# Attention into two gated layers on one core: block transposes moved from TensorE to VectorE and DRAM

## Chip, cores and metric

The kernel runs on one core of one Trainium2 chip. The metric is the device time in microseconds (us) of one execution. Of the kernel before, three runs gave 1791.05, 1791.21 and 1791.79 us; the median is 1791.21.

## What is computed

The inputs are q, k and v of shape (8, 8, 576, 64): batch B, heads H, sequence S, head width D. Linear attention is followed by two feed-forward layers on 4608 tokens of width 512:

```python
q_s = exp(q - max(q, -1)); q_s = q_s / (sum(q_s, -1) + 1e-9)
k_s = exp(k - max(k, 2));  k_s = k_s / (sum(k_s, 2) + 1e-9)
kv  = einsum('bhsd,bhse->bhde', k_s, v)
x   = einsum('bhsd,bhde->bhse', q_s, kv)       # then (B, H, S, D) -> (B*S, H*D)
x   = (silu(x @ w_gate) * (x @ w_val)) @ w_out     # d_ff 1536
out = elu(x @ w_in) @ w_out2                       # d_ff 2048
```

The maximum and the sum over the keys run over the sequence, which lies on partitions in the kernel; the queries' run over the head width, which lies along a partition.

## The kernel before

The tokens are cut into NB = 9 blocks of TB = 512. Every matrix of the feed-forward layers is kept as a high and a low float32r part, and a product is three matmuls (`proj`, lines 617 to 640, and `mm3`, lines 609 to 615). The program has three phases over the nine blocks: "a" (first half of w_gate, w_val, w_out), "b" (second half) and "2" (the second layer).

In phase a, block i has HALF = 6 steps f, and each step has three slots s. Slot 0 is the gate projection, followed on ScalarE (ACT) by the four operations of `silu_act` (lines 660 to 663). Slot 1 is the value projection, with `silu_gate` (lines 667 and 670) and `silu_val` (line 673) on VectorE (DVE). Slot 2 is the w_out product of the step before (`emit_B`). Two PSUM tiles "a" alternate between gate and value, so the gate projection of step f+1 needs line 670 of step f to be done. The low part of the activated tile is line 651 on DVE.

Beside this, block i prepares the attention of block t = i+1. What runs in which slot is written by hand: `PLAN0`, `PLAN1` and `PLAN` (lines 784 to 805) give every step a pair (f, s) for i = 0, i = 1 and i from 2 on; `steps` (line 808) says what a step is; `side_1a` (line 849) issues those of a slot in the order of the plan's text. Each engine, and SP's queue of DMAs, runs in that order of issue. The steps that matter here:

- `load_k`, `load_q`, `load_v` (lines 227 to 265) load keys, queries and values. The values go in five DMAs with rows of 256 bytes (line 242), issued with `kv1`; the queries go in rows of 1024 bytes. A query tile has partition p holding tokens 4p to 4p+3 of the block.
- `kmax` (267) takes the key maximum over the tokens of one partition. `k1` (276) turns it with four TensorE transposes (line 280) into a PSUM bank and reduces it on DVE (284). `k2` (289) broadcasts it back with four transposes (line 293) into another bank, and `ks` (305) subtracts it from the keys. `kexp` (314) takes the exponent on ACT, `kv` (322) multiplies keys and values in 80 small matmuls (line 331) and divides on DVE.
- `qmax`, `qsub`, `qexp`, `qsum`, `qnorm` (350 to 381) make the query softmax. `qnorm` writes the tile `qn` (line 378).
- `qT` (385) turns one pair of heads with four TensorE transposes (line 390) into a bank and copies it on ACT into a tile `qT` (line 398). There are four pairs. `xT` (412) multiplies two pairs with the kv product (`xT_mm`, line 451), copies to the tile x on ACT (433) and takes the low part on DVE (463).
- `store` (468) writes x to DRAM for phase b.

The transposed token order is that of the tile, so `emit_D` writes the output rows as `(p j)` of a block. Lines 390 and 293 and the matmuls of lines 331 and 451 use the two PSUM banks "t" and "c".

Of the kernel before, what the change touches and what calls it, by code (L numbers as in the profile page):

```python
# [17 lines left out]
def kernel(  # L18
# [184 lines left out]
    k_t, q_t, km_t = {}, {}, {}  # L203


    ke = at1.tile([128, 5, H, D], FP32, name="ke")
    start = [True]

# [28 lines left out]
    def load_v(b):  # L237
        for j in range(5):
            n = 128 if j < 4 else NREST
            src = v[b, :, 0:512, :].rearrange("h (p j) d -> p j h d", j=4)[:, j] if j < 4 else \  # L240
                v[b, :, 512:S, :].rearrange("h p d -> p h d")
            nc.sync.dma_start(out=vtile[0:n, j, :, 0:D], in_=src)  # L242


    def load_q(t):
        qt = at1.tile([128, H, 4, D], FP32, tag="q", name="q")
        p0 = min(16 * t, 128)
        s0 = TB * t
        if p0 > 0:
            b = t - 1  # L250
            s = s0 - b * S
            for e in range(2):
                nc.sync.dma_start(
                    out=qt[0:p0, 4 * e:4 * e + 4],
                    in_=q[b, e::2, s:s + 4 * p0, :].rearrange("h (p j) d -> p h (j d)", j=4),
                )
        if p0 < 128:
            b = t
            s = s0 + 4 * p0 - b * S
            for e in range(2):  # L260
                nc.sync.dma_start(
                    out=qt[p0:128, 4 * e:4 * e + 4],
                    in_=q[b, e::2, s:s + 4 * (128 - p0), :].rearrange("h (p j) d -> p h (j d)", j=4),
                )
        q_t[t] = qt

    def kmax(b):
        t, r = k_t[b]
        m = at1.tile([128, H, D], FP32, tag="km", name="km")
        nc.vector.tensor_tensor(m, t[:, :, 0, :], t[:, :, 1, :], op=ALU.max)  # L270
        nc.vector.tensor_tensor(m, m, t[:, :, 2, :], op=ALU.max)
        nc.vector.tensor_tensor(m, m, t[:, :, 3, :], op=ALU.max)
        nc.vector.tensor_tensor(m[0:NREST], m[0:NREST], r, op=ALU.max)
        km_t[b] = m

    def k1(b, meanwhile=None):
        m = km_t[b].rearrange("p h d -> p (h d)")
# [36 lines left out]
    def kexp(b):  # L314
        nc.scalar.activation(out=ke[:, 0:4], in_=ke[:, 0:4], func=ACTF.Exp)
        nc.scalar.activation(out=ke[0:NREST, 4], in_=ke[0:NREST, 4], func=ACTF.Exp)
# [53 lines left out]
    def qnorm(t, n, eng=None):  # L370
        h = slice(4 * n, 4 * n + 4)
        x = q_t[t][:, h]
        r = qr_t[t][:, h]
        nc.vector.tensor_scalar(r, r, 1e-9, None, op0=ALU.add)
        nc.vector.reciprocal(out=r, in_=r)
        if n == 0:
            qn_t[t] = at1.tile([128, 4, H, D], FP32, tag="qn", name="qn")
        (eng or nc.vector).tensor_tensor(
            qn_t[t][:, :, h].rearrange("p j h d -> p h j d"), x,
            r.unsqueeze(3).to_broadcast([128, 4, 4, D]), op=ALU.mult,  # L380
        )

    qT_t = {}

    def qT(t, pair):
        g, e = divmod(pair, 2)
# [54 lines left out]
    def xT_mm(t, g, banks):  # L441
        p0 = min(16 * t, 128)
        for b, c in ((t - 1, slice(0, p0)), (t, slice(p0, 128))):
            if c.start == c.stop:
                continue
            for e in range(2):
                pair = 2 * g + e
                for a, ps in banks.items():
                    r = slice(a * D, (a + 1) * D)
                    o = slice(e * D, (e + 1) * D)  # L450
                    nc.tensor.matmul(  # L451
                        out=ps.rearrange("p (j n) -> p j n", j=4)[o, :, c],
                        lhsT=bds[b % 2][r, pair, :],
                        rhs=qT_t[t, pair].rearrange("p (j n) -> p j n", j=4)[r, :, c],
                        start=True, stop=True,
                    )
        for a, ps in banks.items():
            xT_ps[t, 2 * g + a] = ps
# [285 lines left out]
    def emit_D(i, f):  # L744
        if f == 0:
            acc_tiles(("2", i))
        gt = G.pop((i, f))
        w = W["p", f]
        for j in range(4):
            js = slice(j * 128, (j + 1) * 128)  # L750
            mm3(acc["2", i][j], (gt[:, 0, js], gt[:, 1, js]), (w[:, 0, :], w[:, 1, :]),
                f == 0, f == F2 - 1)
        if f == F2 - 1:
            ev = ev_p.tile([128, KD, TB], FP32, tag="ev", name="ev")
            dst = out[i * TB:(i + 1) * TB, :].rearrange("(p j) n -> p j n", j=4)
            for j in range(4):
                if i == NB - 1 and j == 3:
                    nc.scalar.activation(
                        out=ev[:, j, 0:256], in_=acc["2", i][j][:, 0:256], func=ACTF.Copy
                    )  # L760
                    nc.vector.tensor_copy(ev[:, j, 256:512], acc["2", i][j][:, 256:512])
                elif j % 2 == 0:
                    nc.scalar.activation(out=ev[:, j, :], in_=acc["2", i][j], func=ACTF.Copy)
                else:
                    nc.vector.tensor_copy(ev[:, j, :], acc["2", i][j])
                if i == NB - 1:
                    nc.sync.dma_start(out=dst[:, j], in_=ev[:, j])
            if i < NB - 1:
                nc.sync.dma_start(out=dst, in_=ev)
# [4 lines left out]
    def load_next(ph, i):  # L774
# [7 lines left out]


    PLAN = {
# [4 lines left out]
        "kmax": (4, 2), "qmax": (5, 2),  # L789
    }  # L790
    PLAN0 = {
# [13 lines left out]
        "kmax": (4, 2), "qmax": (5, 2),  # L805
    }

    def steps(i):
        t, u = i + 1, i + 2
        e = nc.gpsimd if i == 0 else nc.vector  # L810
        st = {}
        if i == 1:
            st["store0"] = lambda: store_x(0)
        if t < B:
            st["kmax0"] = lambda: kmax(t)
            st["k1"] = lambda: k1(t)
            st["k2"] = lambda: (k2(t), t + 1 < B and t > 1 and load_k(t + 1))
            st["ks0"] = lambda: ks(t, (0, 1), nc.gpsimd)
            st["ks1"] = lambda: (ks(t, (2, 3), nc.gpsimd), ks(t, (4,), nc.vector))
            st["load_v"] = lambda: load_v(t)  # L820
            st["load_k2"] = lambda: load_k(t + 1)
            st["load_q2"] = lambda: load_q(t + 1)
            st["load_v2"] = lambda: load_v(t + 1)
            st["kexp"] = lambda: kexp(t)
            st["kv0"] = lambda: kv(t, 0)
            st["kv1"] = lambda: (
                kv(t, 1),
                t + 1 < B and t > 1 and load_v(t + 1),
            )
        if t < NB:  # L830
            st["qmax0"] = lambda: (qmax(t, 0), qmax(t, 1))
            st["sub0"] = lambda: qsub(t, 0, e)
            st["sub1"] = lambda: qsub(t, 1, e)
            st["exp0"] = lambda: qexp(t, 0)
            st["exp1"] = lambda: qexp(t, 1)
            st["sum"] = lambda: (qsum(t, 0), qsum(t, 1))
            st["norm0"] = lambda: qnorm(t, 0, e)
            st["norm1"] = lambda: (qnorm(t, 1, e), t + 1 < NB and t > 1 and load_q(t + 1))
            for n in range(KD):
                st[f"qT{n}"] = lambda n=n: qT(t, n)  # L840
                st[f"xT{n}"] = lambda n=n: xT(t, n)
            st["store"] = lambda: store_x(t)
        if u < B:
            st["kmax"] = lambda: kmax(u)
        if u < NB:
            st["qmax"] = lambda: (qmax(u, 0), qmax(u, 1))
        return st
# [90 lines left out]
    with tc.manual_schedule():  # L938
        nc.gpsimd.memset(ident, 1.0)
        nc.gpsimd.affine_select(  # L940
            out=ident, in_=ident, pattern=[[-1, 128]], compare_op=ALU.is_equal, fill=0.0,
            base=0, channel_multiplier=1,
        )
        warm = const.tile([128, 1], FP32, name="warm")
        nc.vector.memset(warm, 0.0)
        nc.scalar.activation(out=warm, in_=warm, func=ACTF.Exp)
        first_block()
        start[0] = False
        run_1()
        run_2()  # L950
# [30 lines left out]
```

## Time and profile before

| | us |
|---|---|
| median of three runs | 1791.21 |
| the profiled execution | 1792.23 |
| its span in the trace | 1790.5 |
| TensorE busy / DVE busy / ACT busy | 1752.0 / 924.9 / 856.0 |

PE is the matmul side of TensorE and PEld its weight loads. Times in rows are us from the start of the span. A timeline row gives start, duration, engine, line, operation, output and inputs with shapes, count, and in brackets the idle time before it with what ended it. A window row gives the busy time of each engine with the number of instructions, then the granted TensorE clock as a share of full speed, the mean busy share of the 16 DMA engines (which can pass 1 where transfers overlap) and GB/s. In a DMA issue row the last number is the median time from issue to landing.

### The profile page before, as it was taken

How to read it: one execution, taken by the hardware profiler on the slowest of the kernel's cores; microseconds unless marked ns; L12 is line 12 of the kernel's file. 1: busy time of each engine (PE TensorE's matmuls, PEld its weight loads, DVE VectorE, ACT ScalarE, POOL GpSimd, SP SyncE). 2: the span in 40 equal slices, each digit the busy share in tenths (PEclk: the TensorE clock that was granted, in tenths of full speed). 3: DMA queues.
4: the chain of work that ended last, by engine and by line, in shares of the span. 5: the costliest groups of instructions: out<-in, count | busy, mean ns of one | idle time of the engine just before them, and what ended most of it. 6: DMA issues, size and time to landing. Idle time of an engine off the chain costs nothing.

```text
span 1790.5 us, 21046 instructions
## 1 busy us (share of the span) xinstructions
PE 1752.0 (98%) x8448; PEld 1433.3 (80%) x8448; DVE 924.9 (52%) x1383; ACT 856.0 (48%) x1466; POOL 173.1 (10%) x135
## 2 busy tenths in 40 slices
PE   6799999999999999999999999999999999999999
PEld 4577888888888888888888788888888888888887
DVE  6866567556577666534346744333433343334343
ACT  4563544534465454433334654444444444444444
POOL 3630000000022222111113300000000000000000
PEclk9899999999999999999999999999999999999999
DMA  9274534341255344433334401010101010101000
GB/s 273 80 228 102 147 100 124 105 114 65 78 192 176 129 171 168 165 118 118 118 118 164 174 3 71 1 71 1 71 1 71 1 71 1 71 1 71 1 24 24
DMA packets 103106, 169.13 MB, mean 94 GB/s; under 512 B 41696, under 2 KB 80608, under 8 KB 98528
## 3 DMA queue, kind: packets, MB, share of 16 engines
q1 hardware_dynamic: 103008, 167.79, 28.5%
q8 instruction: 66, 1.08, 0.3%
q14 instruction: 32, 0.26, 0.0%
HBM read 111.15 MB, written 56.62 MB: 94 GB/s over the span
## 4 chain that ended last, share of the span: by engine, by line
PE 90%; issue 2%; DVE 2%; POOL 2%; ACT 2%; DMA 1%; SPq 1%; POOLq 0%; DVEq 0%; ACTq 0%
PE a L632 17%; PE a L633 17%; PE a L636 17%; PE y L613 12%; PE y L615 12%; PE y L614 12%; POOL w L183 1%; PE t L451 1%; DMA ev<-in_v 1%; PE t L390 1%; SPq L242 0%; PE t L331 0%; PE c L331 0%; DMA xs<-x 0%; POOL ke L310 0%
## 5 line engine op out<-in xcount | busy, mean ns | idle before, releaser
L632 PE MATMUL a<-x,w 128*128 128x512 f32 x1432 | 562.8, 393 | 1.5 <-DVE th L688 1.2
L633 PE MATMUL a<-x,w 128*128 128x512 f32 x1432 | 558.9, 390 | 0.7 <-POOL x L463 0.7
L636 PE MATMUL a<-x,w 128*128 128x512 f32 x1432 | 382.8, 389 | 0.0
L645 ACT ACTIVATE g<-th 128x512 fp32r<-128x512 f32 x252 | 159.3, 632 | 442.4 <-DVE th L673 226.3
L632 PEld LDWEIGHTS a<-x,w 128*128 128x128 f32 x1432 | 269.8, 188 | 60.7 <-DVE th L688 2.0
L633 PEld LDWEIGHTS a<-x,w 128*128 128x128 f32 x1432 | 269.8, 188 | 56.2 <-POOL x L463 1.2
L636 PEld LDWEIGHTS a<-x,w 128*128 128x128 f32 x1432 | 268.8, 188 | 55.8
L685 DVE SCALAR_TENSOR_TENSOR th<-e,th 128x512 f32<-128x512 f32 x144 | 100.9, 701 | 356.6 <-ACT e L684 356.6
L651 DVE TENSOR_TENSOR g<-th,g 128x512 fp32r<-128x512 f32 x246 | 176.2, 716 | 136.7 <-ACT g L645 136.6
L613 PE MATMUL y<-w,g 128*128 128x512 f32 x576 | 224.1, 389 | 0.0
L615 PE MATMUL y<-w,g 128*128 128x512 f32 x576 | 224.1, 389 | 0.0
L614 PE MATMUL y<-w,g 128*128 128x512 f32 x576 | 224.1, 389 | 0.0
L667 DVE SCALAR_TENSOR_TENSOR th<-th,e 128x512 f32<-128x512 f32 x108 | 77.3, 715 | 274.6 <-ACT th L663 274.6
L682 ACT ACTIVATE e<-a 128x512 f32<-128x512 f32 x144 | 86.1, 598 | 183.4 <-PE a L636 183.4
L613 PE MATMUL y<-g,w 128*128 128x512 f32 x432 | 171.8, 398 | 0.0
L660 ACT ACTIVATE e<-a 128x512 f32<-128x512 f32 x107 | 64.1, 599 | 224.4 <-PE a L636 224.3
L614 PE MATMUL y<-g,w 128*128 128x512 f32 x432 | 169.0, 391 | 0.0
L615 PE MATMUL y<-g,w 128*128 128x512 f32 x432 | 169.0, 391 | 0.0
L183 POOL TENSOR_TENSOR w<-cd,w 128x512 fp32r<-128x512 f32 x68 | 91.6, 1349 | 624.8 <-ACT w L182 604.1
L613 PEld LDWEIGHTS y<-w,g 128*128 128x128 f32 x576 | 108.2, 188 | 22.6
L615 PEld LDWEIGHTS y<-w,g 128*128 128x128 f32 x576 | 108.1, 188 | 22.5
L614 PEld LDWEIGHTS y<-w,g 128*128 128x128 f32 x576 | 108.1, 188 | 22.3
(137 smaller groups left out, 1705.7 us busy)
## 6 DMA issues: line engine op xcount, KB each, us to landing
xs<-x SPq DMA_DIRECT2D x9, 2048.0 KB, 6.3
x<-xs SPq DMA_DIRECT2D x36, 512.0 KB, 6.2
ys<-yst SPq DMA_DIRECT2D x36, 512.0 KB, 3.7
x<-ys SPq DMA_DIRECT2D x36, 512.0 KB, 7.2
raw<-in_moe_w_out SPq DMA_DIRECT2D x26, 512.0 KB, 3.3
yp<-ev SPq DMA_DIRECT2D x9, 1024.0 KB, 4.0
ev<-yp SPq DMA_DIRECT2D x9, 1024.0 KB, 7.9
raw<-in_moe_w_in SPq DMA_DIRECT2D x16, 512.0 KB, 4.0
```

The lines of the kernel that those rows point to most:

```text
L183: eng.tensor_tensor(w[:, 1, :], df, w[:, 0, :].bitcast(FP32), op=ALU.subtract)
L613: nc.tensor.matmul(out=ps, lhsT=wh, rhs=xh, start=first, stop=False)
L614: nc.tensor.matmul(out=ps, lhsT=wh, rhs=xl, start=False, stop=False)
L615: nc.tensor.matmul(out=ps, lhsT=wl, rhs=xh, start=False, stop=last)
L632: nc.tensor.matmul(out=ps, lhsT=wh, rhs=x[:, c, 0, :], start=(c == 0), stop=False)
L633: nc.tensor.matmul(out=ps, lhsT=wh, rhs=x[:, c, 1, :], start=False, stop=False)
L636: nc.tensor.matmul(out=ps, lhsT=wl, rhs=x[:, c, 0, :], start=False, stop=(c == KD - 1))
L645: nc.scalar.activation(out=gt[:, 0, :], in_=src, func=ACTF.Copy)
L651: (eng or nc.vector).tensor_tensor(gt[:, 1, :], src, gt[:, 0, :].bitcast(FP32), op=ALU.subtract)
L667: nc.vector.scalar_tensor_tensor(out=t, in0=t, scalar=1.0, in1=e, op0=ALU.add, op1=ALU.mult)
L682: nc.scalar.activation(out=e, in_=h, func=ACTF.Relu, scale=-1.0)
L685: nc.vector.scalar_tensor_tensor(out=t, in0=e, scalar=1.0, in1=t, op0=ALU.add, op1=ALU.mult)
```

## The change

From block TURN = 3 on, TensorE does no transposes for the attention.

- Queries: `qnorm` now scales in place. `qturn` turns 32x32 squares of the query tile on DVE, two instructions of 128x512 elements for each half of the heads, and writes them so that the token order is natural. `qout` writes the tile to a DRAM tensor `dq` in four DMAs, each from 32 partitions with rows of 512 bytes, 1 MB in all. `qin` reads two pairs at a time back as tiles `qT`, two DMAs of 256 KB with rows of 2 KB. `xT_mm` uses plain column slices for these blocks.
- Key maxima: `kturn` turns the 128x512 tile on DVE into a PSUM bank, reduces, turns again, copies and reduces again on DVE, writes 16x32 values to DRAM and reads them back broadcast to 128 partitions.
- `PLAN` is written anew: the softmax of the queries and keys moves up by one to three slots, `turn1` (which issues `qout`, `qin(t, 0)` and the next query load) stands in slot (2, 0) behind `kv1`, `xT0` and `xT1` stay in (3, 1), `in1` follows them there, and `xT2` and `xT3` move from (4, 1) to (4, 2). The copies of line 398, the second PSUM tile of the key maxima and lines 280, 293 and 390 are gone for these blocks.
- `emit_D` writes rows of blocks 3 to 8 as `(j p)`.

```diff
+    TURN = 3
+    NQ = 32
+    dq = {t: dr.tile([KD, 4, NQ, 4, 128], FP32, name=f"dq{t}") for t in range(TURN, NB)}
+    dk = {b: dr.tile([2 * H, NQ], FP32, name=f"dk{b}") for b in range(TURN, B)}
...
+    def kturn(b):
+        m = km_t[b].rearrange("p h d -> p (h d)")
+        ps = bank()
+        nc.vector.transpose(ps, m)
+        nc.vector.tensor_reduce(
+            out=kq[:, 0:2 * H], in_=ps.rearrange("p (x c) -> p x c", c=NQ), axis=AX.X, op=ALU.max
+        )
+        nc.vector.transpose(kt_, kq)
+        for g in range(4):
+            nc.vector.tensor_copy(kc[:, g], kt_[g * NQ:g * NQ + 2 * H])
+        mk = at2.tile([2 * H, NQ], FP32, tag="mk", name="mk")
+        nc.vector.tensor_reduce(
+            out=mk, in_=kc.rearrange("p g r -> p r g"), axis=AX.X, op=ALU.max
+        )
+        nc.sync.dma_start(out=dk[b], in_=mk)
+        mb = at1.tile([128, H, D], FP32, tag="km", name="mb")
+        nc.sync.dma_start(
+            out=mb.rearrange("p h d -> p (h d)"),
+            in_=dk[b].rearrange("x r -> (x r)").unsqueeze(0).to_broadcast([128, H * D]),
+        )
+        km_t[b] = mb
...
+        if t >= TURN:
+            nc.vector.tensor_tensor(
+                x, x, r.unsqueeze(3).to_broadcast([128, 4, 4, D]), op=ALU.mult
+            )
+            return
...
+    def qturn(t, n):
+        if n == 0:
+            qn_t[t] = at1.tile([128, 2 * H, 128], FP32, tag="qn", name="qn")
+        h = slice(4 * n, 4 * n + 4)
+        for e in range(2):
+            o = qn_t[t].rearrange("p (h e) (c j) -> p h e j c", e=2, j=4)[:, h, e]
+            nc.vector.transpose(o, q_t[t][:, h, :, e * NQ:(e + 1) * NQ])
+
+    def qout(t):
+        for g in range(4):
+            nc.sync.dma_start(
+                out=dq[t].rearrange("s q r g n -> r (s q) g n")[:, :, g],
+                in_=qn_t[t][g * NQ:(g + 1) * NQ],
+            )
+
+    def qin(t, g):
+        for e in range(2):
+            x = at2.tile([128, 512], FP32, tag="qT", name="qT")
+            nc.sync.dma_start(
+                out=x, in_=dq[t][2 * e + g].rearrange("q r g n -> (q r) (g n)")
+            )
+            qT_t[t, 2 * g + e] = x
...
     PLAN = {
-        "k1": (0, 1), "k2": (1, 0), "kexp": (1, 0), "kv0": (2, 0), "kv1": (2, 0),
-        "sub0": (0, 2), "exp0": (0, 2), "sub1": (0, 2), "exp1": (0, 2), "sum": (1, 2), "norm0": (2, 1), "norm1": (2, 2),
-        "qT0": (3, 0), "qT1": (3, 0), "xT0": (3, 1), "xT1": (3, 1),
-        "qT2": (4, 0), "qT3": (4, 0), "xT2": (4, 1), "xT3": (4, 1), "store": (5, 0),
-        "kmax": (4, 2), "qmax": (5, 2),
+        "sub0": (0, 0), "exp0": (0, 0), "sub1": (0, 0), "exp1": (0, 0),
+        "ks": (0, 2), "kexp": (0, 2), "sum": (1, 0), "norm0": (1, 1), "norm1": (1, 2),
+        "turn0": (1, 2), "kv0": (2, 0), "kv1": (2, 0), "turn1": (2, 0),
+        "xT0": (3, 1), "xT1": (3, 1), "in1": (3, 1), "xT2": (4, 2), "xT3": (4, 2), "store": (5, 1),
+        "kmax": (4, 1), "kturn": (4, 2), "qmax": (5, 2),
     }
...
+            st["ks"] = lambda: (
+                ks(t, range(5), nc.vector), t + 1 < B and load_k(t + 1),
+            )
...
-            st["norm1"] = lambda: (qnorm(t, 1, e), t + 1 < NB and t > 1 and load_q(t + 1))
+            st["norm1"] = lambda: (qnorm(t, 1, e), t + 1 < NB and t == 2 and load_q(t + 1))
+            st["turn0"] = lambda: qturn(t, 0)
+            st["turn1"] = lambda: (
+                qturn(t, 1), qout(t), qin(t, 0), t + 1 < NB and load_q(t + 1),
+            )
+            st["in1"] = lambda: qin(t, 1)
```

`PLAN1` gets `"kturn": (5, 0)`. In `kv1` the next value load stays as it was, for t from 2 to 6.

## Rows read from the trace of the kernel before

**Rows 1.** The page, parts 1 and 4: busy times, and shares of the chain.

```profile
span 1790.5 us, 21046 instructions
...
PE 1752.0 (98%) x8448; PEld 1433.3 (80%) x8448; DVE 924.9 (52%) x1383; ACT 856.0 (48%) x1466; POOL 173.1 (10%) x135
...
PE 90%; issue 2%; DVE 2%; POOL 2%; ACT 2%; DMA 1%; SPq 1%; POOLq 0%; DVEq 0%; ACTq 0%
```

**Rows 2.** Windows, one block of phase a (i = 4) nearly whole.

```profile
297.00:354.00 57.00, 57.00 (x354) 46.28 (x353) 35.70 (x57) 26.90 (x47) 0.00 (x0) 1.00 0.41 117
```

**Rows 3.** Timeline of PE in that block, from step f = 2 to step f = 3.

```profile
300.84 0.39 PE L632 MATMUL a<-x,w 128*128 128x512 f32 x1
...
311.72 0.39 PE L632 MATMUL a<-x,w 128*128 128x512 f32 x1
...
313.53 1.07 PE L636 MATMUL a<-x,w 128*128 128x512 f32 x4
314.44 0.60 PE L390 MATMUL c<-ident,qn 128*128 128x128 f32 x4
...
317.16 1.07 PE L636 MATMUL a<-x,w 128*128 128x512 f32 x4
318.15 0.48 PE L451 MATMUL t<-qT,bd 64*64 64x320 f32 x1
```

**Rows 4.** Timeline of ACT: the ends of three gate projections, steps 5, 0 and 2.

```profile
392.18 0.60 ACT L660 ACTIVATE e<-a 128x512 f32<-128x512 f32 x1 [2.47 <-PE a L636]
400.34 0.60 ACT L660 ACTIVATE e<-a 128x512 f32<-128x512 f32 x1 [3.13 <-PE a L636]
...
417.60 0.60 ACT L660 ACTIVATE e<-a 128x512 f32<-128x512 f32 x1 [2.33 <-PE a L636]
```

**Rows 5.** Timeline of DVE: qnorm to the next product, and the key subtractions.

```profile
365.10 0.17 DVE L374 TENSOR_SCALAR qr<-qr 128x16 f32<-128x16 f32 x1
...
366.73 0.68 DVE L673 SCALAR_TENSOR_TENSOR th<-th,a 128x512 f32<-128x512 f32 x1
...
409.40 2.48 DVE L310 TENSOR_TENSOR ke<-k,t 128x512 f32<-128x512 f32 x4 [1.42 <-PE t L293]
411.80 0.67 DVE L312 TENSOR_TENSOR ke<-kr,t 64x512 f32<-64x512 f32 x1
```

**Rows 6.** Timeline of SP's queue: the value load of block i = 4.

```profile
305.78 4.20 SPq L242 DMA_DIRECT2D vtile<-in_v  x5
```

**Rows 7.** Windows: values; their end; queries from 32 partitions; keys.

```profile
310.50:311.00 0.50, 0.50 (x4) 0.42 (x3) 0.43 (x3) 0.47 (x1) 0.00 (x0) 1.00 1.34 218
312.00:312.50 0.50, 0.50 (x4) 0.42 (x3) 0.50 (x2) 0.00 (x0) 0.00 (x0) 1.00 0.97 124
316.50:317.00 0.50, 0.50 (x4) 0.42 (x3) 0.21 (x1) 0.50 (x2) 0.00 (x0) 1.00 1.08 219
358.00:359.00 1.00, 1.00 (x6) 0.84 (x5) 1.00 (x2) 0.35 (x1) 0.00 (x0) 1.00 1.08 386
```

**Rows 8.** The page, part 6: DMA issues to and from DRAM.

```profile
xs<-x SPq DMA_DIRECT2D x9, 2048.0 KB, 6.3
...
raw<-in_moe_w_out SPq DMA_DIRECT2D x26, 512.0 KB, 3.3
yp<-ev SPq DMA_DIRECT2D x9, 1024.0 KB, 4.0
```

**Rows 9.** Waits of PE (total us, times, longest), early in the run.

```profile
PE t L331 <- ACT ke L315: 3.1, 1, 3.1
...
PE t L390 <- ACT xf L436: 1.2, 1, 1.2
```

**Rows 10.** Windows: after the 3.1 us wait, and around the 1.2 us wait.

```profile
76.00:80.00 4.00, 4.00 (x32) 3.30 (x30) 2.55 (x4) 4.00 (x9) 3.13 (x3) 0.57 0.00 0
98.00:100.00 2.00, 0.87 (x6) 0.83 (x7) 0.69 (x1) 1.25 (x3) 2.00 (x2) 1.00 1.14 241
```

More of the change, by code (lines that the diff above doesn't have):

```diff
@@ L203 @@
     k_t, q_t, km_t = {}, {}, {}
+    TURN = 3
+    NQ = 32
+    dq = {t: dr.tile([KD, 4, NQ, 4, 128], FP32, name=f"dq{t}") for t in range(TURN, NB)}
+    dk = {b: dr.tile([2 * H, NQ], FP32, name=f"dk{b}") for b in range(TURN, B)}
+    kq = at1.tile([128, NQ], FP32, name="kq")
+    kt_ = at1.tile([128, NQ], FP32, name="kt")
+    kc = at1.tile([2 * H, 4, NQ], FP32, name="kc")
     ke = at1.tile([128, 5, H, D], FP32, name="ke")
@@ L450, in xT_mm @@
                     o = slice(e * D, (e + 1) * D)
+                    x = qT_t[t, pair]
+                    if t >= TURN:
+                        c4 = slice(4 * c.start, 4 * c.stop)
+                        out_, rhs = ps[o, c4], x[r, c4]
+                    else:
+                        out_ = ps.rearrange("p (j n) -> p j n", j=4)[o, :, c]
+                        rhs = x.rearrange("p (j n) -> p j n", j=4)[r, :, c]
                     nc.tensor.matmul(
[L452 to L455, printed above, removed]
+                        out=out_, lhsT=bds[b % 2][r, pair, :], rhs=rhs, start=True, stop=True,
                     )
@@ L754, in emit_D @@
             ev = ev_p.tile([128, KD, TB], FP32, tag="ev", name="ev")
-            dst = out[i * TB:(i + 1) * TB, :].rearrange("(p j) n -> p j n", j=4)
+            dst = out[i * TB:(i + 1) * TB, :]
+            if i >= TURN:
+                dst = dst.rearrange("(j p) n -> p j n", j=4)
+            else:
+                dst = dst.rearrange("(p j) n -> p j n", j=4)
             for j in range(4):
@@ L804 @@
         "qT2": (4, 0), "qT3": (4, 1), "xT2": (4, 2), "xT3": (4, 2), "store": (5, 2),
-        "kmax": (4, 2), "qmax": (5, 2),
+        "kmax": (4, 2), "kturn": (5, 0), "qmax": (5, 2),
     }
@@ L844, in steps @@
             st["kmax"] = lambda: kmax(u)
+            st["kturn"] = lambda: kturn(u)
         if u < NB:
@@ L945 @@
         nc.vector.memset(warm, 0.0)
+        nc.vector.memset(kq, 0.0)
         nc.scalar.activation(out=warm, in_=warm, func=ACTF.Exp)
```

## The prediction

> **What bounds the kernel now.** I read the page first: PE is busy 1752.0 of 1790.5 us and carries 90% of the chain that ended last, while DVE is busy 52% and ACT 48% [rows 1]. Shares are averages, so the next view is the windows of one block of phase a: PE is busy for the whole 57 us, DVE for 35.7, and the granted clock is 1.00 [rows 2]. In this stretch every instruction taken from PE shortens the run, and every wait put in front of PE lengthens it; DVE and ACT have room. So the timeline of PE tells the gain, and the queue of SP and the windows of the DMA engines tell what the replacement costs. Waits that PE had early in the run tell what an idle PE costs beyond the idle time.
>
> **What is removed.** Eight transposes of line 390 stand between two projections. Undisturbed, a projection takes 1.81 us from its first matmul to its group of line 636 (311.72 to 313.53), and that group .91 more. Here the transposes start at 314.44 and the next group of line 636 at 317.16, 2.72 later, so the eight transposes with their switch cost 2.72 - 1.81 = 0.91 us [rows 3]. Two such groups per block make 1.82, and blocks t = 3 to 8 make 6 x 1.82 = 10.9 us. For the key maxima I compare steps: a step without side work takes 392.18 to 400.34 = 8.16 us; steps 0 and 1 together, which hold the transposes of lines 280 and 293, take 400.34 to 417.60 = 17.26, so these cost 17.26 - 16.32 = 0.94 [rows 4]. Keys b = 3 to 7 make 4.7 us. Together 15.6 us, all of it on the path. The ACT copies of line 398 that go too were not on it.
>
> **What DVE gets.** No row shows a DVE transpose. Line 310 starts four operations of 128x512 in 2.40 us, 0.60 each [rows 5]; I take that for each of the four turns of a block, with twice as much as upper bound (two passes for 4-byte data can't be excluded) and nothing below 0.3 as lower. That is 2.4 us per block, and about 2.5 us for `kturn`, against 0.7 for line 284. DVE has 57.0 - 35.7 = 21 us free in a block [rows 2], so in total this costs nothing. Its place does: if line 670 comes late, the next gate projection waits. The tightest place is step 1, where the exponents of the keys on ACT now stand ahead of the gate's four operations; I work out a lateness of 1.2 us there against a margin of 1.6, so nothing, and at most 0.5 per block if the estimate is off. The end of the second turn follows from the same ledger, taken in the times of the block of [rows 3]: line 670 of step 1 ends its slot at 300.3 (estimate, with the lateness of 1.2); then qnorm 1.63, line 673 0.60, qnorm 1.63 [rows 5], first turn 1.2, line 651 0.6, kv 1.2 and the second turn 1.2 end at 308.4.
>
> **What the round trip costs.** This is the step that decides. `xT` of pairs 0 and 1 stood at 318.15, after eight transposes that go: PE now wants these tiles at 318.15 - 0.91 = 317.24 [rows 3]. They come through four writes that SP issues after `turn1`, a wait of SP until all four have landed, and two reads. Queued behind this wait on SP is the next query load, which has some 20 us of room and costs nothing. In front of the writes, though, stands the value load of `kv1`: SP issues its five DMAs from 305.78 to 309.98 [rows 6], and the DMA engines move them at 218 GB/s until about 312.4 [rows 7]. All of SP's DMAs go through one queue, so in the four blocks t = 3 to 6 the write's data begins at 312.4, whatever DVE does. For the data of 1 MB the bounds are 2.3 us (a store of 2 MB lands in 6.3 us, one of 1 MB in 4.0 [rows 8]) and 4.8 us (219 GB/s, queries going to 32 partitions, like each of these writes, or rows of 256 bytes [rows 7]). Rows of 512 bytes lie between the 256 bytes of the values at 218 and the 1024 of the keys at 386 GB/s [rows 7], some 300, or 3.5 us; I take 4.2, midway between this and the 32-partition row. Of the 4.0 us of a 1 MB store 2.3 are data; 1.4 of the rest go by before the first byte and 0.3 after the last (estimate). So the writes land at 312.4 + 4.2 + 0.3 = 316.9. The reads bring 512 KB together; a 512 KB load takes 3.3 us [rows 8], 2.9 at best. With 0.1 for the semaphore the tiles are there at 320.3: PE stands for 3.1 us, in four blocks.
>
> Block t = 7 has no value load behind `kv1`: 308.4 + 1.4 + 4.2 + 0.3 + 3.4 = 317.7, a stall of 0.5. Block t = 8 has neither kv nor key work: PE wants the tiles 2.7 earlier, at 314.5, the second turn ends at 305.9, and the tiles come at 315.2, a stall of 0.7. The second reads (`in1`) have some 11 us until `xT2` and are hidden; so is the key maxima's trip, which has some 12 us until `ks`, and the output rows, which are written by transfers that nothing waits for except the last one, with the same row size as before.
>
> **What a stall costs beyond itself.** Early in the run PE waited 3.1 us for line 315 and, elsewhere, 1.2 us for line 436 [rows 9]. After the first the granted clock over 76 to 80 us averaged 0.57, falling to the lower of its two levels, 1.2 GHz; after the second it stayed at 1.00 [rows 10]. The loss in those four us is 4 x 0.43 = 1.7 us of full-speed work. I add it to each stall of 3.1 and not to those under 1.2.
>
> **The sum.** Blocks t = 3 to 6: each 3.1 + 1.7 - 1.82 - 0.94 = +2.0, together +8.2. Block 7: 0.5 - 2.76 = -2.3. Block 8: 0.7 - 1.82 = -1.1. Net +4.8 us. The profiled execution took 1792.23 us, 1790.5 of span and 1.7 around it; its time is 1.0 above the median of the runs. On the median: 1791.2 + 4.8 = 1796.0 us.
>
> The Trainium skill, page "DMA: Bandwidth & Descriptors", section "Anatomy of one DMA", prices a transfer at about 2.0 us plus its bytes at 436 GB/s. As an estimate from that page, the 1 MB out would take 4.4 us and the 512 KB back 3.2, and behind the value load PE would stall some 0.7 us instead of 3.1. The trace agrees for long rows (4.0 us for 1 MB), and disagrees for rows of 256 bytes, which ran at half that rate [rows 7]. It stands beside the first rival.
>
> **Rivals.** First, the trip is fast enough: the writes run like the x store and reads like the quickest load. Then the tiles come at 312.4 + 2.3 + 0.3 + 3.0 = 318.0, a stall of 0.8 in four blocks, none in the last two, no loss of clock: 1791.2 - 15.6 + 3.2 = 1778.8. At the keys' rate (2.7) and with 3.3 for the reads the stall is 1.6 and the time 1782.0. It decides as soon as the write's 1 MB takes under about 3 us. For it speaks that stores here have long rows and run well; against it, that every transfer from or to few partitions, or in short rows, ran near 220 GB/s. Chance 0.31.
>
> Second, the stall is as forecast but the clock stays up: -15.6 + 4 x 3.1 + 0.5 + 0.7 = -2.0, or 1789.2, no change that can be told. The wait of 1.2 us speaks for it, the one of 3.1 against it [rows 9, 10]. Chance 0.13.
>
> Third, DVE's turns take 1.2 us each: the second turn ends at 310.8, which blocks 3 to 6 hardly feel, but blocks 7 and 8 stall 2.9 and 3.1 and lose the clock too, 4.1 us more each: 1804. Chance 0.08. That the change doesn't do what it says, that is, that the transposes cost PE nothing, is excluded as far as the rows of PE go.
>
> **Numbers.** The forecast has 0.48. A measurement of this kernel can tell a change of over about 0.2% (3.6 us) from none. Faster by more than that are the first rival and a little of the second, 0.33; within it, most of the second and the low edge of the forecast, 0.15; slower, the rest of the forecast and the third, 0.52. The range takes the first rival's lower end and the third's: 1779 to 1805; the forecast's own, with 3.5 to 4.8 us for the data, is 1792 to 1800.
>
> **What would show it.** In the new trace, line 451 should wait for a DMA of `qT` from `dq`, some 3 us in each of blocks 3 to 6 and under 1.2 in 7 and 8; the granted clock should fall after the former. The writes to `dq` should begin their traffic only when the values' has ended. Blocks 7 and 8 should be shorter than before, blocks 3 to 6 longer. A DVE transpose should take about 0.6 us per 512 elements. I am wrong if line 451 waits under 2 us, or if the writes overtake the value load.

## The result and the profile after

The changed kernel takes 1807.68 us (median of 4 runs, 1806.48 to 1813.85) against 1791.43 for the kernel before (4 runs beside them): a ratio of 1.0097, 95% interval 1.0085 to 1.0108. It is 16.3 us slower, where 4.8 were forecast. The profiled execution took 1807.69.

In the changed kernel line 451 of the kernel before, the product of queries and kv, is line 519; the transposes of line 390 (now line 451) are left only for the first blocks. Lines 632, 633, 636 are now 697, 698, 701; 614 is 679; 651 is 716; 660 is 725; 667, 670, 673 are 732, 735, 738; 242 is 251. New are 289 to 302 (`kturn`), 429 (`qturn`), 433 (`qout`) and 441 (`qin`).

The page of the changed kernel, parts 1 and 4, answering to [rows 1]:

```profile
span 1806.0 us, 20889 instructions
...
PE 1747.2 (97%) x8312; PEld 1422.8 (79%) x8312; DVE 957.7 (53%) x1443; ACT 843.6 (47%) x1442; POOL 173.2 (10%) x135
...
PE 80%; DVE 9%; ACT 4%; DMA 3%; issue 1%; SPq 1%; POOL 1%; DVEq 0%; ACTq 0%; POOLq 0%
```

PE has 136 instructions fewer, yet its busy time is only 4.8 us down (some of its matmuls now run at a lower clock), and the span is 15.5 us longer. DVE's share of the chain went from 2% to 9%, the DMAs' from 1% to 3%. So time is lost in front of PE. The view of PE's waits in the changed kernel (engine, tile and line, who was waited for: total us, times, longest) says where:

```profile
PE t L519 <- DMA qT<-dq: 18.3, 6, 3.8
...
PE y L679 <- DVE g L716: 2.3, 4, 0.6
...
PE a L697 <- DVE th L735: 1.1, 1, 1.1
```

In the kernel before the first two don't occur, and the third (line 670 there) was 0.3 us. Their places are in the timeline of PE, one row for each of the blocks t = 3 to 8 (and one of the four waits for line 716):

```profile
207.33 0.34 PE L519 MATMUL t<-qT,bd 64*64 64x192 f32 x1 [3.55 <-DMA qT<-dq]
...
267.68 0.40 PE L519 MATMUL t<-qT,bd 64*64 64x256 f32 x1 [3.09 <-DMA qT<-dq]
...
327.41 0.45 PE L519 MATMUL t<-qT,bd 64*64 64x320 f32 x1 [3.82 <-DMA qT<-dq]
...
349.19 0.50 PE L679 MATMUL y<-g,w 128*128 128x512 f32 x1 [0.51 <-DVE g L716]
...
387.77 0.50 PE L519 MATMUL t<-qT,bd 64*64 64x384 f32 x1 [3.12 <-DMA qT<-dq]
...
445.60 0.56 PE L519 MATMUL t<-qT,bd 64*64 64x448 f32 x1 [2.05 <-DMA qT<-dq]
...
500.64 0.61 PE L519 MATMUL t<-qT,bd 64*64 64x512 f32 x1 [2.64 <-DMA qT<-dq]
```

What a stall costs in all is read from the ends of the gate projections, the timeline of ACT, here of the block that prepares t = 5 (steps 3, 4, 5 and the next 0):

```profile
320.90 0.60 ACT L725 ACTIVATE e<-a 128x512 f32<-128x512 f32 x1 [2.21 <-PE a L701]
336.36 0.60 ACT L725 ACTIVATE e<-a 128x512 f32<-128x512 f32 x1 [3.11 <-PE a L701]
345.76 0.60 ACT L725 ACTIVATE e<-a 128x512 f32<-128x512 f32 x1 [0.83 <-PE a L701]
354.77 0.60 ACT L725 ACTIVATE e<-a 128x512 f32<-128x512 f32 x1 [2.86 <-PE a L701]
```

The step with `xT0` and `xT1` takes 336.36 - 320.90 = 15.46 us; the one with `xT2` and `xT3`, which has the same matmuls and no wait, 9.40. In the blocks t = 3 to 8 that step takes 15.19, 13.30, 15.46, 13.21, 12.37 and 14.25: 27.4 us more than six of 9.40, of which 18.3 are idle. The other 9.1 follow the stalls, in part as a lower clock. Windows of the changed kernel, right behind the stalls of t = 5, 6 and 8 (columns as in [rows 2]; the first number after POOL's is the granted clock):

```profile
328.00:331.00 3.00, 3.00 (x17) 1.61 (x16) 0.30 (x1) 0.93 (x2) 0.00 (x0) 0.50 1.02 256
...
387.80:391.00 3.20, 3.20 (x23) 2.00 (x24) 0.87 (x2) 1.09 (x2) 0.00 (x0) 1.00 0.98 258
...
500.60:504.00 3.40, 3.36 (x12) 1.76 (x13) 0.91 (x2) 1.09 (x2) 0.00 (x0) 0.70 0.33 91
```

After 3.82 us idle PE ran at the lower level, 1.2 GHz (0.50); after 3.12 it kept 2.4 GHz; after 2.64 the mean is 0.70. The clock fell in t = 3, 5 and 8 and stayed up in 4, 6 and 7. A step in which it fell cost 2.2 us beyond its idle time, one in which it stayed 0.7 to 0.9.

The last step of the rows above, 354.77 - 345.76 = 9.01 us, was 8.16 before [rows 4]. It follows `kturn`, and its like comes in the blocks t = 3 to 6: 0.85 to 0.94 each, 3.6 us. Timeline of DVE in the changed kernel:

```profile
345.69 0.71 DVE L289 STREAM_TRANSPOSE t<-km 128x512 f32<-128x512 f32 x1
...
348.46 0.67 DVE L716 TENSOR_TENSOR g<-th,g 128x512 fp32r<-128x512 f32 x1
```

From its first operation to line 716 the chain holds DVE for 2.8 us, and line 716, which the w_out product needs, stands behind it: the wait of 0.51 at 349.19.

### The profile page after: what moved, and what is told of

It reads as the page before. It is cut to its first block, busy times and chain, and to the rows that moved or that the text cites. A ratio compares the mean times of both kernels' runs of the same rounds, so it can differ in the third digit from the quotient of the medians.

```text
span 1806.0 us, 20889 instructions
## 1 busy us (share of the span) xinstructions
PE 1747.2 (97%) x8312; PEld 1422.8 (79%) x8312; DVE 957.7 (53%) x1443; ACT 843.6 (47%) x1442; POOL 173.2 (10%) x135
## 4 chain that ended last, share of the span: by engine, by line
PE 80%; DVE 9%; ACT 4%; DMA 3%; issue 1%; SPq 1%; POOL 1%; DVEq 0%; ACTq 0%; POOLq 0%
PE a L697 15%; PE a L698 15%; PE a L701 15%; PE y L679 11%; PE y L678 11%; PE y L680 11%; DMA dq<-qn 1%; PE t L519 1%; DMA qT<-dq 1%; DVE qn L429 1%; DVE th L732 1%; DVE th L735 1%; ACT ke L347 1%; SPq L433 1%; DMA ev<-in_v 1%
```

## Experiments

Theory A is that PE waits for the round trip of the queries, and that the trip is long in itself: slow turns, a slow write, then reads. Its rival, the prediction's own view, is that the trip is late because the value load goes ahead of it. A second question is what `kturn` costs.

**Give the trip more time.** `xT0` and `xT1` stand two slots later, the rest of the chain with them:

```diff
-        "xT0": (3, 1), "xT1": (3, 1), "in1": (3, 1), "xT2": (4, 2), "xT3": (4, 2), "store": (5, 1),
+        "xT0": (4, 0), "xT1": (4, 0), "in1": (4, 0), "xT2": (5, 1), "xT3": (5, 1), "store": (5, 2),
```

> xT0, xT1 and in1 move from slot (3, 1) to (4, 0), xT2 and xT3 to (5, 1), store to (5, 2); nothing else. Theory A (PE waits for the round trip, and each wait also costs clock and a slow restart): the waits of line 519 for qT go from 18.3 us to under 1, the lower clock and the restart go too, so some 18.3 + 5 + 4 = 27 us less than the changed kernel: about 1780 us. Rival B (DVE and the DMA traffic of the turns are what costs, the wait only shows it): the wait moves to another line, and the time stays above 1795.

Measured: 1776.42 us (4 runs, 1775.73 to 1778.38) against 1791.74, ratio 0.9919 (0.9905 to 0.9934). The span is 1774.0 us. No wait of line 519 is left. Of this kernel, the timeline of ACT in the same stretch (steps 3, 4, 5 and 0), then windows:

```profile
308.00 0.60 ACT L725 ACTIVATE e<-a 128x512 f32<-128x512 f32 x1 [2.22 <-PE a L701]
316.16 0.60 ACT L725 ACTIVATE e<-a 128x512 f32<-128x512 f32 x1 [3.13 <-PE a L701]
325.57 0.60 ACT L725 ACTIVATE e<-a 128x512 f32<-128x512 f32 x1
334.97 0.60 ACT L725 ACTIVATE e<-a 128x512 f32<-128x512 f32 x1 [2.47 <-PE a L701]
```

```profile
205.00:262.00 57.00, 57.00 (x345) 45.85 (x347) 41.67 (x68) 24.64 (x43) 0.00 (x0) 1.00 0.62 169
```

The step that took 15.46 takes 8.16 now that `xT` has left it, the two that hold `xT` take 9.41 and 9.40, and PE is busy all the time at full clock. A block is 2.75 us shorter than before, as the prediction's saving of 1.82 + 0.94 says. The saving is there; the changed kernel asks for the tiles too early. What is left of the change's other costs is the lateness of `kturn` in block 1 (PE waits 1.1 us for line 735 as in the change). This version beats both kernels: 15.3 us faster than before, some 31 faster than the change.

**Only one slot later.** `xT0`, `xT1`, `in1` to (3, 2), the rest as in the change.

```diff
-        "xT0": (3, 1), "xT1": (3, 1), "in1": (3, 1), "xT2": (4, 2), ...
+        "xT0": (3, 2), "xT1": (3, 2), "in1": (3, 2), "xT2": (4, 2), ...
```

> xT0, xT1 and in1 move by one slot only, to (3, 2); xT2 and xT3 stay in (4, 2). Theory A: the slot gives 2.72 us, so of the six waits of line 519 (18.3 us) some 0.5 is left in each of blocks 3 to 6 and none in 7 and 8, and the clock stays up; kturn's 3.6 us remain. 1776.4 + 2 + 1.5 for restarts + 3.6 = 1783 to 1785.

Measured: 1787.97 (10 runs, 1786.45 to 1792.2) against 1791.47, ratio 0.9982 (0.9973 to 0.9992): a miss of some 3 us. Line 519 still waits 5.0 us in all (1.12, 1.05, then 1.15 and 1.44 in one block, 0.21), and the lateness behind `kturn` is still there: its step takes 8.97 to 9.10. The trip is late by more than one slot, and `xT` has to move past more than one.

**The value load behind the first reads.**

```diff
-                t + 1 < B and t > 1 and load_v(t + 1),
+                t + 1 < B and t == 2 and load_v(t + 1),
...
-                qturn(t, 1), qout(t), qin(t, 0), t + 1 < NB and load_q(t + 1),
+                qturn(t, 1), qout(t), qin(t, 0), t + 1 < B and load_v(t + 1),
+                t + 1 < NB and load_q(t + 1),
```

> Only the value load moves on SP's queue, from in front of the writes to dq to behind the first reads (blocks 3 to 6). Theory A1 (the writes' own data and the two landings make the wait; the value load costs only what is left of it when DVE has turned): the wait of blocks 3 to 6 falls from some 3.4 us to that of block 7, 2.1, about 1807.7 - 4 x 1.3 = 1802, and up to 5 us less again where the clock stays up. Rival, as the prediction had it (the value load in front of the writes is what makes the wait): the wait of blocks 3 to 6 falls under 1 us, 1793 or less.

Measured: 1803.95 (1802.97 to 1806.51), ratio 1.0076 (1.0059 to 1.0093). SP's queue in the block t = 5, and PE's waits, of this kernel:

```profile
313.99 3.43 SPq L433 DMA_DIRECT2D dq<-qn  x4
321.06 0.81 SPq L441 DMA_DIRECT2D qT<-dq  x2
321.97 4.87 SPq L251 DMA_DIRECT2D vtile<-in_v  x5
```

```profile
PE t L519 <- DMA qT<-dq: 16.3, 7, 2.9
```

With nothing ahead of it the trip is still late, by 2.2 to 2.9 us in every block: SP needs 3.43 us to issue the four writes, and 7.07 pass from the first issue to the reads. Moving the value load takes 0.6 to 1.5 us off each of the four stalls (3.55, 3.09, 3.82 and 3.12 become 2.88, 2.45, 2.37 and 2.19) and 3.7 off the kernel, though `xT2` of t = 4 now waits 1.31. In the prediction it was worth 2.6 a block, the difference between 3.1 and the 0.5 of block 7. So the value load is a part of the stall, not the whole.

Why it is worth so little can be read in the changed kernel. Timeline of DVE, the second turn of t = 6:

```profile
375.04 1.99 DVE L429 STREAM_TRANSPOSE qn<-q 128x512 f32<-128x512 f32 x2
```

It ends at 377.03, and SP issues the first write at 377.62, just behind the value load. In t = 3 to 6 only 0.4 to 1.1 us lie between the two, so without the value load the writes can't start much earlier.

**What makes the write slow.** Two kernels write the same 1 MB in four DMAs another way, with the rearrangement left out, and the reads wait for all four, as in the change. One uses 128 partitions with four rows of 512 bytes each:

```diff
-                out=dq[t].rearrange("s q r g n -> r (s q) g n")[:, :, g],
-                in_=qn_t[t][g * NQ:(g + 1) * NQ],
+                out=dq[t].rearrange("s q r g n -> s (q r g) n").rearrange(
+                    "s (c p) n -> c p s n", p=128)[g],
+                in_=qn_t[t][:, 4 * g:4 * g + 4],
```

> As e5 (four writes, each from 128 partitions, rows of 512 bytes, the rearrangement left out), but each write reaches into all four parts of dq, so that the first reads wait for all four writes again, as in the changed kernel. e5 had let them wait for one write each. If the 32 partitions are what slows the write (e5's traffic: 288 GB/s against 175), the four land 5 us after the first issue instead of 7.0 and the wait of line 519 in block 7 falls from 2.05 to about 0.2; if e5's gain came from the fewer waits, it stays near 2.

The other keeps 32 partitions and makes the rows 8 KB:

```diff
-                out=dq[t].rearrange("s q r g n -> r (s q) g n")[:, :, g],
-                in_=qn_t[t][g * NQ:(g + 1) * NQ],
+                out=dq[t].rearrange("s q r g n -> (s q r g n)").rearrange(
+                    "(a c x) -> c a x", c=4, x=2048)[g],
+                in_=qn_t[t][g * NQ:(g + 1) * NQ].rearrange("p h n -> p (h n)"),
```

> As e6 (32 partitions, one row of 8 KB each, the rearrangement left out), but the first reads wait for all four writes. If 32 partitions alone limit the write, the traffic stays near 175 GB/s and the wait of block 7 near 2; if short rows add to it, the traffic is some 250 GB/s as in e6 and the wait of block 7 about 0.8.

Measured, one run each beside 1791.47 for the kernel before: 1792.86 and 1799.24. Line 519 (520 here) waits 9.7 us, nothing of it in t = 7 and 8, and 13.2 us, of it 1.12 in t = 7 and 1.76 in t = 8. The block t = 8, SP's queue and then windows of the write: first of the changed kernel, then of the one with 128 partitions, then SP's queue of the one with long rows.

```profile
490.80 3.42 SPq L433 DMA_DIRECT2D dq<-qn  x4
497.92 4.89 SPq L441 DMA_DIRECT2D qT<-dq  x4
```

```profile
492.00:493.00 1.00, 1.00 (x6) 0.84 (x5) 0.70 (x2) 0.16 (x1) 0.00 (x0) 1.00 1.00 176
493.00:494.00 1.00, 1.00 (x7) 0.81 (x6) 0.50 (x1) 0.47 (x1) 0.00 (x0) 1.00 1.01 172
```

```profile
478.59 3.33 SPq L433 DMA_DIRECT2D dq<-qn  x4
484.35 5.72 SPq L442 DMA_DIRECT2D qT<-dq  x4
```

```profile
480.00:481.00 1.00, 1.00 (x6) 0.82 (x5) 1.00 (x3) 0.00 (x0) 0.00 (x0) 1.00 1.03 295
...
482.00:483.00 1.00, 1.00 (x6) 0.84 (x5) 0.90 (x2) 0.00 (x0) 0.00 (x0) 1.00 1.06 286
```

```profile
484.54 2.71 SPq L433 DMA_DIRECT2D dq<-qn  x4
490.62 0.81 SPq L442 DMA_DIRECT2D qT<-dq  x2
```

From the first write's issue to the reads' issue: 7.12 us in the change, 5.76 from 128 partitions, 6.08 with long rows. At the same row length, with the DMA engines at a busy share of about 1.0 in all four windows, 32 partitions move 172 to 176 GB/s and 128 move 286 to 295. Over the whole write the engines are busy for 5.5 us (window by window, 491 to 498), 192 GB/s for the 1 MB, and for 3.8 (479 to 484), 275 GB/s; two later windows of the first ran at 184 and 232. In the second there is a gap of about 0.5 us between the second and the third write; that SP's issue has become the slower part there is likely, not shown. With long rows from 32 partitions the engines are busy for 4.5 us (485 to 490). The partitions are worth 1.36 us of the trip, the row length 1.04. The Trainium skill, page "SBUF — State Buffer", section "Door 1: The DMA port swizzle", says that a transfer's rate depends on how many of 16 ports its partitions reach, and that partitions 0 to 31 reach half of them (189 GB/s at 1 MiB, against 328 for all 128). The windows roughly agree in the ratio, with 172 to 176 against 286 to 295, at somewhat lower rates (each write here is 256 KB, with four under way).

Two earlier kernels with the same two shapes gave each write to one `s` alone, so that the reads waited for fewer writes each.

```diff
-                out=dq[t].rearrange("s q r g n -> r (s q) g n")[:, :, g],
-                in_=qn_t[t][g * NQ:(g + 1) * NQ],
+                out=dq[t].rearrange("s q r g n -> s (q r g n)").rearrange(
+                    "s (c p n) -> s p c n", p=128, n=128)[g],
+                in_=qn_t[t][:, 4 * g:4 * g + 4],
...
-                out=dq[t].rearrange("s q r g n -> r (s q) g n")[:, :, g],
-                in_=qn_t[t][g * NQ:(g + 1) * NQ],
+                out=dq[t][g].rearrange("q r g n -> (q r g n)").rearrange("(r x) -> r x", r=NQ),
+                in_=qn_t[t][g * NQ:(g + 1) * NQ].rearrange("p h n -> p (h n)"),
```

> Each of the four writes to dq takes 128 partitions with four rows of 512 bytes each instead of 32 partitions with sixteen; same bytes, same number of rows. It leaves out the rearrangement (rows land in other places of dq), so the queries are not those of the reference. Theory P (few partitions limit the write): issue to landing of all four falls from 7.0 us to about 5, and the wait of line 519 in block 7 from 2.05 to under 0.5. Theory R (rows of 512 bytes limit it): unchanged, 7 us and 2 us.

> Each of the four writes still takes 32 partitions, but one row of 8 KB each instead of sixteen of 512 bytes. It leaves out the rearrangement too. Theory R: the four land some 4 to 4.5 us after the first issue, SP issues them in under 2 us instead of 3.4, and the wait of block 7 goes. Theory P: unchanged, 7 us and 2 us.

They took 1785.63 and 1792.74 (one run each), with waits of 3.0 and 6.7 us. They mix the shape with the shorter wait and settle nothing on the shape. Against the kernel before beside them they stand at -6.2 and +0.9 us, the two above at +1.4 and +7.8: the shorter wait goes with 7.6 and 6.9 us, from one run each.

**The turn itself.** The turn writes a square's columns side by side (with tokens out of order) instead of 16 bytes apart.

```diff
-            o = qn_t[t].rearrange("p (h e) (c j) -> p h e j c", e=2, j=4)[:, h, e]
+            o = qn_t[t].rearrange("p (h e) (j c) -> p h e j c", e=2, j=4)[:, h, e]
```

> The changed kernel, but the DVE turns of the queries write their 32 columns side by side instead of 16 bytes apart (the token order of the result is wrong by that). If the stride of the writes makes the 1.11 us of line 429, it falls to the 0.71 us of kturn's 128x512 turn (line 289); if it is the 4-byte turn itself, it stays at 1.1.

Measured: 1803.8, one run. The group of line 429 (busy us, mean ns of one), in the changed kernel:

```profile
L429 DVE STREAM_TRANSPOSE qn<-q 128x512 f32<-128x512 f32 x24 | 24.7, 1110 | 0.0
```

and in this one, with the two rows of PE for t = 7 and 8:

```profile
L429 DVE STREAM_TRANSPOSE qn<-q 128x512 f32<-128x512 f32 x24 | 15.5, 685 | 0.0
```

```profile
444.79 0.56 PE L519 MATMUL t<-qT,bd 64*64 64x448 f32 x1 [0.85 <-DMA qT<-dq]
...
498.28 0.61 PE L519 MATMUL t<-qT,bd 64*64 64x512 f32 x1 [1.38 <-DMA qT<-dq]
```

Of 1.11 us, 0.43 are due to the stride of the writes. In t = 7 and 8 the stall falls by 1.20 and 1.26; in t = 3 to 6 it does not change (3.65, 3.12, 3.51, 3.08), because SP comes to the writes only after the value load's issue there (in t = 6 the load's five DMAs are issued from 373.56 to 377.93, the first write at 378.01). Together with the run that moved the value load, this says that in t = 3 to 6 the turn and the value load each hide the other; a kernel with both taken away was not run.

**Key maxima earlier**, three to four slots ahead of the place where DVE is short:

```diff
-        "kmax": (4, 1), "kturn": (4, 2), "qmax": (5, 2),
+        "kmax": (3, 0), "kturn": (3, 2), "qmax": (5, 2),
```

and `"kturn": (5, 1)` instead of (5, 0) in `PLAN1`.

> Only the key maxima move: kmax from (4, 1) to (3, 0) and kturn from (4, 2) to (3, 2), in block 1 kturn from (5, 0) to (5, 1). Theory A says that kturn stands in front of the low part of step 4 (line 716) and of the gate of step 5, and that PE waits for it 0.85 us in each of four blocks and 1.4 in block 1: 4.8 us less than the changed kernel, 1803. Rival B (it is the DVE time itself, wherever it stands): no change.

Measured: 1809.26 (1808.35 to 1812.82), ratio 1.0105 (1.009 to 1.012), a miss. The step behind `kturn` is back at 8.16, as expected. In block 1 only 0.2 us of the 1.4 come back (three steps of 25.76 us, 25.95 in the change). But line 519 waits 19.1 us, and now the clock falls in five blocks of six instead of three. Of this kernel, the stalls of t = 7 and 8, then windows behind them:

```profile
447.52 0.56 PE L519 MATMUL t<-qT,bd 64*64 64x448 f32 x1 [2.35 <-DMA qT<-dq]
...
503.89 0.61 PE L519 MATMUL t<-qT,bd 64*64 64x512 f32 x1 [2.65 <-DMA qT<-dq]
```

```profile
449.00:451.00 2.00, 2.00 (x9) 1.40 (x6) 0.65 (x2) 1.08 (x2) 0.00 (x0) 0.50 0.99 320
...
506.00:508.00 2.00, 2.00 (x10) 1.65 (x9) 1.81 (x3) 0.64 (x2) 0.00 (x0) 1.00 0.81 268
```

The step of t = 7 took 14.00 us, 2.25 beyond 9.40 and its idle time; that of t = 8 took 12.67, 0.6 beyond. The six steps together are 5.6 us longer than in the change, which eats the some 4 us gained. The time of a kernel with such stalls depends on where the clock falls, and that can differ from run to run: of the changed kernel one of the four runs took 1813.85 us at a mean granted clock of 0.986, the others 1806.48 to 1807.69 at 0.993. So the two kernels can't be told apart by their times; the lateness gone behind `kturn` is read from the steps.

**Both moves together:**

> e1 and e2 together. Theory A: 15.6 us of transposes saved and none given back, 1791.4 - 15.6 = 1776. Rival B: above 1785.

Measured: 1777.11 (1776.08 to 1777.77), ratio 0.9921 (0.9906 to 0.9936), no better than the later `xT` alone. With `xT2` and `xT3` in step 5, no wait for line 716 is left even at the old place of `kturn`, so moving it has nothing to gain there.

**Each half of the change alone.** First the queries alone, in the plan with the later `xT`; the keys go through PE again:

```diff
-        if b == 1:
+        if b == 1 or b >= TURN:
...
-        "kmax": (4, 1), "kturn": (4, 2), "qmax": (5, 2),
+        "kmax": (3, 0), "kturn": (3, 1), "kback": (3, 2), "qmax": (5, 2),
```

with `kturn` issuing `k1` and `kback` issuing `k2`.

> The later xT of e1, but the key maxima of batches 3 to 7 are turned and broadcast by TensorE again (k1 in slot (3, 1), k2 with a copy on ACT in (3, 2), kmax in (3, 0); in block 1 in (5, 1) and (5, 2)). If the key part of the change is worth the 0.94 us of PE per batch that it removes, this takes 4.7 us more than e1 (1776.4), less some 1.5 that kturn costs in block 1: 1779 to 1781. If it is worth nothing, 1776 to 1777.

Measured: 1781.34 (5 runs, 1780.22 to 1783.0), ratio 0.994 (0.9926 to 0.9953). That is 10.5 us under the kernel before (1791.84 beside it), where the version with both halves was 15.3 under it, so the keys are worth 4.8, give or take the 2 to 3 us by which runs of one kernel differ. The steps agree: the one with `k1` and `k2` takes 9.09 us against 8.16, 0.93 a block. The prediction had 10.9 for the queries and 4.7 for the keys.

Then the keys alone, in the changed plan, with the queries on PE (slots (3, 0) and (4, 0) again):

```diff
-        if t >= TURN:
+        if t >= 99:
...
-        "turn0": (1, 2), "kv0": (2, 0), "kv1": (2, 0), "turn1": (2, 0),
+        "kv0": (2, 0), "kv1": (2, 0), "qT0": (3, 0), "qT1": (3, 0), "qT2": (4, 0), "qT3": (4, 0),
```

The first edit stands in `qnorm`, in `xT_mm` and, for i, in `emit_D`, and the next query load is issued with `norm1` again.

> The plan of the changed kernel, but the queries are turned by TensorE as before (qT0 and qT1 in (3, 0), qT2 and qT3 in (4, 0)); only the key maxima go through DVE and DRAM. Theory A: 4.7 us saved and about 5 given back by kturn in front of line 716 and of the gate of step 5: 1791.5, no change. If the key part pays in this plan: 1787.

Measured: 1787.57 (10 runs, 1787.14 to 1788.68), ratio 0.9977 (0.9968 to 0.9987), 4 us better than expected. The step behind `kturn` takes 8.19 here: the lateness is gone with `kturn` at the same place. So it is not `kturn` alone that costs 3.6 us in the change. Of this kernel, the timelines of ACT, DVE and PE, the block t = 5:

```profile
323.62 0.60 ACT L725 ACTIVATE e<-a 128x512 f32<-128x512 f32 x1 [2.47 <-PE a L701]
...
335.74 0.67 DVE L716 TENSOR_TENSOR g<-th,g 128x512 fp32r<-128x512 f32 x1
...
336.67 0.40 PE L679 MATMUL y<-g,w 128*128 128x512 f32 x1
```

Line 716 ends 12.8 us after the gate operation in both kernels (336.41 - 323.62 here, 349.13 - 336.36 in the change). PE comes to line 679 after 13.05 us here; in the change it had run out of work after 12.32 (349.19 - 0.51 - 336.36). As long as PE turns the queries in that step, it has work of its own while DVE runs the chain; without that work it gets to line 679 earlier and waits. Only the lateness in block 1 stays.

## Why the prediction was wrong

The direction and the mechanism were right: PE loses less than 16 us of work and gets a wait for the queries' way through DRAM, with a lower clock behind it. The size was not. In the prediction's own terms:

| term | forecast | measured |
|---|---|---|
| transposes saved | -15.6 | -15.6 (12 steps 0.91 shorter, 5 pairs of steps 0.94) |
| stalls and clock, t = 3 to 6 | +19.2 | +19.6 |
| stall, t = 7 | +0.5 | +3.0 |
| stall, t = 8 | +0.7 | +4.8 |
| `kturn` | 0 | +5.1 |
| sum | +4.8 | +16.9 |

The stalls are the excess of the six steps over 9.40, idle time and what follows it; the saving is read from the steps without a wait, 10.31 before and 9.40 after, and 17.26 before and 16.32 after for steps 0 and 1 together. The sum can also be read directly: between two gate operations on ACT that start at 102.64 and 510.60 us before, and at 102.38 and 527.14 after, the kernel became 424.76 - 407.96 = 16.8 us longer; the other 1.3 us of difference to the span's 15.5 lie outside this stretch and were not looked into.

**The step that failed is the length of the trip where no value load goes ahead of it** (blocks 7 and 8; 6.6 us of the 12.1 that the sums differ by). Block 7: PE wants the tile at 445.60 - 2.05 = 443.55. SP's queue in the changed kernel, blocks t = 6 and t = 7, then DVE's two turns of t = 7:

```profile
373.11 4.41 SPq L251 DMA_DIRECT2D vtile<-in_v  x5
377.62 3.79 SPq L433 DMA_DIRECT2D dq<-qn  x4
385.01 0.82 SPq L441 DMA_DIRECT2D qT<-dq  x2
...
435.95 3.41 SPq L433 DMA_DIRECT2D dq<-qn  x4
443.00 0.81 SPq L441 DMA_DIRECT2D qT<-dq  x2
```

```profile
430.18 2.15 DVE L429 STREAM_TRANSPOSE qn<-q 128x512 f32<-128x512 f32 x2
...
433.95 1.97 DVE L429 STREAM_TRANSPOSE qn<-q 128x512 f32<-128x512 f32 x2
```

- The second turn was to end 317.24 - 308.4 = 8.84 us ahead of that; the writes were issued 7.60 ahead, 1.24 late. The turn of 0.60 taken from a DVE product measured 1.11, within the bounds, near the upper one. A pair of them was to take 1.2 and takes 2.0 (430.18 to the next operation at 432.15, and 433.95 to 435.92): two pairs make 1.5, and the rest of the ledger came out 0.3 earlier. The value of the nearest shape of work was taken, and it said nothing of a write with 16 bytes between elements.
- The write was to take 1.4 + 4.2 + 0.3 = 5.9; it took 7.05. The data are the reason, at a rate held down by the 32 partitions and by the rows of 512 bytes (1.36 and 1.04 us of the trip in the two runs on the write's shape). The row of 219 GB/s for queries to 32 partitions [rows 7] was quoted as a bound of 4.8 us of data and then averaged with a faster one; even that bound was short, as the data alone took 5.5 us in t = 8. The price from the Trainium skill that the prediction set beside its first rival (page "DMA: Bandwidth & Descriptors", section "Anatomy of one DMA") is given there for transfers issued by GpSimd, while SP issues all of these; its 4.4 us for the 1 MB was further off than the prediction's own sum.
- The reads were to take 3.4 and took 2.60.

1.24 + 1.15 - 0.80 = 1.6, the difference between 2.05 and 0.5. For t = 8 the same three are 1.4, 1.2 and -0.7. The third rival, slow turns, had seen the first of these terms and put blocks 7 and 8 at 2.9 and 3.1 with the clock lost, which came out nearest to what these blocks did; it had 0.08.

**Blocks 3 to 6 came out right partly by luck.** The writes' data was to wait for the end of the value load, 4.84 us ahead of PE's need, and then take 4.5. In t = 6 SP issued the first write right behind the value load's last, 7.03 us ahead of the need (384.65), only 0.6 later than in t = 7; the write itself took 7.39. The stalls of 3.1 to 3.8 stand where 3.1 was forecast, but moving the value load away left 2.2 to 2.9 of them: the slow turns and the slow write, which the sum had too short, hold the trip up nearly as long as the value load does. The prediction's sign for this cause, that the writes' traffic begins only when the values' has ended, can't be told from the windows there, since the two kinds of traffic follow without a gap.

**The clock** was to fall in four blocks at 1.7 us each and in none with a stall under 1.2. It fell in three, one of them block 8 after 2.64 us, for 2.2 beyond the idle time; and where it stayed up, a stall still cost 0.7 to 0.9 more than itself, which had no term. In the sum of t = 3 to 6 these errors nearly cancel, which is luck: 6.8 forecast, 6.0 measured.

**`kturn` at nothing** was the other failed step. Its 2.5 us on DVE were sized well (2.8), and the danger of a late DVE was named, but at step 1. It came at step 5, where line 716 stands behind the chain, and in block 1, where line 735 does: a wait of 1.11 us, and 1.5 in all (three steps of 25.95 us, against 25.42 before less the 0.94 of the transposes). The work of PE that would have covered the chain was just what the other half of the change takes away, as the run with the keys alone shows.

The saving, the one term worked out wholly from rows of PE, was right: the steps give 0.91 and 0.94, as forecast. The whole kernels agree within their spread: 1791.2 - 15.6 without any stall would be 1775.6, and the version without stalls took 1776.42, with the lateness in block 1 still in it.

## What to carry to other kernels

When work moves from the engine that bounds the kernel into a round trip, count that trip end to end (last producer, issue of each DMA on its queue, data at the rate of that partition count and row length, landing, reads) and put the consumer behind it by slots of the plan: here two slots turned 16 us of loss into 15 of gain, with the same instructions. Price a cover with the change already made: work that hid a side chain before may be the very work that the change removes. And where a stall is left, count more than its idle time: here a stall cost 0.6 to 0.9 us beyond it where the granted clock stayed at 1.00, and 2 to 3.2 where it fell (the change and the kernel with the earlier key maxima).

## What the runs showed of the hardware that was not expected

- A DVE transpose of 128x512 fp32 in 32x32 squares took 685 ns with the squares' columns written side by side, 1110 ns with elements 16 bytes apart.
- A write to DRAM from 32 partitions with 512-byte rows ran at 172 to 176 GB/s in the windows shown (192 over the whole 1 MB), from 128 partitions at 286 to 295 (275), at a busy share of the DMA engines of about 1.0 in both.
- The granted clock does not follow the length of a single stall alone: it fell after 2.64 us idle (mean 0.70 right behind it) and not after 3.12 (1.00) in the changed kernel; in the one with the earlier key maxima it fell after 2.35 (0.50) and not after 2.65 (1.00).
